# Read-out transpose at step 6 in place of step 3, and a batch's two fp32 subtractions on VectorE in place of GpSimd

## The chip, the core and the metric

One core of one Trainium2 chip. The metric is device time in microseconds of one execution; a version's time is the median of several. The engines are named as in the profile: PE is TensorE (PEld its weight loads), DVE is VectorE, ACT is ScalarE, POOL is GpSimd, SP the engine whose queue issues most of the output transfers and all transposing ones.

## What is computed

Eight batches of cross attention between 512 rows `x` and 32 rows `state` (8 heads of 64), both ways, and a two-layer network with an exact GELU on all 544 rows of each batch:

```python
def _attn_ref(x, state):                       # x [8,8,512,64], state [8,8,32,64]
    a  = softmax(scale * x @ state.T)          # per batch and head
    xread = a @ state                          # 512 rows
    a2 = softmax(scale * state @ x.T)
    sread = a2 @ x                             # 32 rows
    return concat([xread, sread], axis=2)

def _moe_ref(x, w_in, w_out):                  # x [4352,512], w_in [512,2048], w_out [2048,512]
    h = x @ w_in
    g = 0.5 * h * (1.0 + erf(h / sqrt(2)))
    return g @ w_out
```

(The softmax divides by the sum plus 1e-9 after the maximum is subtracted.) Inputs and output are fp32.

## The kernel before

**The 512 rows.** The read of the state and the first layer are joined: `P = state @ w_in` per batch (`p_mm`, `p_copy`), then `hp = A.T @ P` (`mm1`), with A.T made by a transposing DMA (`atr_dma`, tile AT). ScalarE applies the GELU and writes `g`.

**The second layer** of batches 2 to 7 uses seven products of half-size blocks for the eight of a plain one. The blocks' sums are made by VectorE (`g_sum` for the inputs, `w_sums` for the weights); the seven products are `X(b, name)`, in the order 3, 6, 4, 5, 1, 2, 7, each sixteen matmuls at line 586, and their results are combined with fp32 additions and subtractions: `s3` and `s34` (from 3 and 4), `q` (from 1), `u = s34 - [5]` at line 634, `v = q - [2]` at line 605 (inside `c22`), then `[6] + v` at line 608 and `[7] + u` at line 642 give half of the output columns each. ScalarE copies the results of 5 and 2 out of PSUM (lines 632, 636) straight into the output tile `oh`, from which `u` and `v` read them. `x_out(b, 1)` and `x_out(b, 0)`, 512 KB each, leave through SP's queue. The four PSUM banks of `ps_o` are shared by these results and by `p_ps` of the next batch: `p_run` of step 5 writes banks 0 and 1 and then 3 and 2, the banks that lines 608 and 642 read last.

**The 32 rows.** `sread` forms them with matmuls from the unnormalized exponentials and the rows in `xo` (which carry a column of ones); `sread_out` divides by the sum and writes `srm`; `srt(b)` transposes `srm` on TensorE (tile srT, line 402) and VectorE copies it into XSR (line 405), strided by batch. `mm1_sr`, in round 7 from step 3 on, needs XSR of all batches; its second layer is done by `R(name)` in the same seven products, with rows of all batches at once, and its own `r_u` and `r_v` at lines 721 and 727.

**The rows' layouts.** GpSimd loads a batch's rows (`load_x`), copies them into `x4` (`rearr`, line 218) for the transposing DMA of `xtr_dma`, and into `xo` (`rearr_ones`, line 228). xo of batch b+2 replaces that of batch b, so it waits for the `sr` matmuls of batch b.

**Order.** It is written out by hand: each engine runs its instructions in the program's order. The last loop runs rounds b = 2 to 7 of eight steps p. In round b, step p: two `mm1` of batch b in each step; the product X of batch b-1 in the order 4, 5, 1, 2, 7 at steps 0 to 4 (rounds 3 to 7); the scores of batch b+1 and `sread(b)` at step 1; the normalization `norm` of batch b+1 (the tile `a`, line 347) at steps 2 and 3; `srt(b)` at step 3, ahead of the `mm1` of that step; `atr_dma(b+1)` at step 5; P of batch b+1 at steps 5 and 7; X 3 and 6 of batch b at steps 6 and 7. On GpSimd, in a round: `load_x(b+3)` and the `x4` copies of batch b+2 at step 0, `u` at step 1, the `xo` copies of batch b+2 at step 2, `v` at step 3. `load_x` stops after batch 7, so in round 5 the `x4` copies are not held back by a load ahead of them. On SP, in a round: xT of batch b+2, the two x_out of batch b-1, AT of batch b+1.

After the loop come X 4, 5, 1, 2 of batch 7 interleaved with the seven R products, and last `X7_split`, which does product 7 in two halves and sends each half out as soon as line 662 has added `u`.

The pools that matter: `ps_f` has four PSUM slots (tag f) for hp, scores, sr, srT and some p_ps; `cpool` has one buffer for each of s3, s34, q, u, v; `hpool` one for each half of the output.

Of the kernel before, what the change touches and what calls it, by code (L numbers as in the profile page):

```python
# [12 lines left out]
ALU = mybir.AluOpType  # L13
# [4 lines left out]
def kernel(  # L18
# [8 lines left out]
    nc = tc.nc  # L27

    B, H, S, D = x.shape
# [25 lines left out]
    def otile(shape, name, at=None):  # L55
        if at is None:
            at = turn[0] % 4
            turn[0] += 1
        return ps_o.tile(shape, FP32, name=name, tag=f"o{at}")

    def ftile(shape, name):
        return ps_f.tile(shape, FP32, name=name, tag="f")
# [479 lines left out]
    NH = d_model // 2  # L542
# [22 lines left out]
    xs = {}  # L565
# [8 lines left out]
    def g_q(b, h, k):  # L574
        return gs[b][:, MH * k:MH * k + MH, 256 * h:256 * h + 256]
# [19 lines left out]
    def c_tile(name):  # L595
        return cpool.tile([128, 2, NH], FP32, name=name, tag=name)

    def x_out(b, h):
        rows = out[b * SB:b * SB + S, :].rearrange("(p j) n -> p j n", j=SJ)
        nc.sync.dma_start(out=rows[:, 2 * h:2 * h + 2, :], in_=xs[b, "o", h])  # L600

    def c22(b):
        xs[b, "v"] = c_tile("v")
        o = xs[b, "o", 1]
        nc.gpsimd.tensor_tensor(  # L605
            out=xs[b, "v"], in0=xs[b, "q"], in1=o[:, :, :NH], op=ALU.subtract
        )
        nc.vector.tensor_tensor(out=o[:, :, NH:], in0=xs[b, 3], in1=xs[b, "v"], op=ALU.add)
        x_out(b, 1)

    def X(b, name):
        bank = {"3": 0, "4": 1, "5": 0, "2": 1, "1": 2, "6": 3, "7": 2}[name]
        first = name in "3416"
        if first:
            xs[b, bank] = otile([128, 2, NH], "xp", bank)
        ps = xs[b, bank]
        lhs = {"3": (0, 0), "4": (1, 1)}.get(name)
        lhs = xs[b, "g" + name] if lhs is None else g_q(b, *lhs)
        rhs = {"5": w_q[1][1], "2": w_q[0][0]}.get(name)
        rhs = w_sum[name] if rhs is None else rhs  # L620
        x_mm(ps, lhs, rhs, first)
        if name == "3":
            xs[b, "s3"] = c_tile("s3")
            nc.scalar.copy(out=xs[b, "s3"], in_=ps)
            for h in range(2):
                xs[b, "o", h] = hpool.tile([128, 2, d_model], FP32, name="oh", tag=f"oh{h}")
        elif name == "4":
            xs[b, "s34"] = c_tile("s34")
            nc.vector.tensor_tensor(out=xs[b, "s34"], in0=ps, in1=xs[b, "s3"], op=ALU.add)  # L629
        elif name == "5":  # L630
            o = xs[b, "o", 0][:, :, NH:]
            nc.scalar.copy(out=o, in_=ps)  # L632
            xs[b, "u"] = c_tile("u")
            nc.gpsimd.tensor_tensor(out=xs[b, "u"], in0=xs[b, "s34"], in1=o, op=ALU.subtract)  # L634
        elif name == "2":
            nc.scalar.copy(out=xs[b, "o", 1][:, :, :NH], in_=ps)  # L636
            c22(b)
        elif name == "1":
            xs[b, "q"] = c_tile("q")
            nc.vector.tensor_tensor(out=xs[b, "q"], in0=ps, in1=xs[b, "s34"], op=ALU.add)  # L640
        elif name == "7":
            nc.vector.tensor_tensor(
                out=xs[b, "o", 0][:, :, :NH], in0=ps, in1=xs[b, "u"], op=ALU.add
            )
            x_out(b, 0)
# [10 lines left out]
    def X7_split(b):  # L656
        rows = out[b * SB:b * SB + S, :].rearrange("(p j) n -> p j n", j=SJ)
        o = xs[b, "o", 0]
        for j in range(2):
            ps = xs[b, "x", j]  # L660
            x_mm(ps, xs[b, "g7"], w_sum["7"], False, (j,))
            nc.vector.tensor_tensor(
                out=o[:, j, :NH], in0=ps[:, 0, :], in1=xs[b, "u"][:, j, :], op=ALU.add
            )
            eng = nc.scalar if j else nc.sync
            eng.dma_start(out=rows[:, j, :NH], in_=o[:, j, :NH])

    rs = {}

    def r_q(h, k):  # L670
        return g_sr[:, MH * k:MH * k + MH, 128 * h:128 * h + 128]
# [16 lines left out]
    def R(name):  # L688
        def c_new(n):
            rs[n] = cpool.tile([128, NH], FP32, name="r_" + n, tag="r_" + n)  # L690
            return rs[n]

        bank = {"3": 0, "4": 1, "5": 0, "2": 1, "1": 2, "6": 3, "7": 2}[name]
        first = name in "3416"
        if first:
            rs[bank] = ftile([128, NH], "rp")
        ps = rs[bank]
        lhs = {"3": (0, 0), "4": (1, 1)}.get(name)
        lhs = rs["g" + name] if lhs is None else r_q(*lhs)
        rhs = {"5": w_q[1][1], "2": w_q[0][0]}.get(name)  # L700
        rhs = w_sum[name] if rhs is None else rhs
        for m in range(MH):
            nc.tensor.matmul(  # L703
                ps,
                lhsT=lhs[:, m, :],
                rhs=rhs[:, m, :],
                start=(first and m == 0),
                stop=(m == MH - 1),
                skip_group_check=True,
            )  # L710
        add, sub = ALU.add, ALU.subtract
        if name == "3":
            nc.scalar.copy(out=c_new("s3"), in_=ps)
            for h in range(2):
                rs["o", h] = opool.tile([128, d_model], FP32, name="osb", tag="osb")
        elif name == "4":
            nc.vector.tensor_tensor(out=c_new("s34"), in0=ps, in1=rs["s3"], op=add)
        elif name == "5":
            o = rs["o", 0][:, NH:]
            nc.scalar.copy(out=o, in_=ps)  # L720
            nc.gpsimd.tensor_tensor(out=c_new("u"), in0=rs["s34"], in1=o, op=sub)
        elif name == "1":
            nc.vector.tensor_tensor(out=c_new("q"), in0=ps, in1=rs["s34"], op=add)
        elif name == "2":
            o = rs["o", 1][:, :NH]
            nc.scalar.copy(out=o, in_=ps)
            nc.gpsimd.tensor_tensor(out=c_new("v"), in0=rs["q"], in1=o, op=sub)
        elif name == "6":
            nc.vector.tensor_tensor(out=rs["o", 1][:, NH:], in0=ps, in1=rs["v"], op=add)
            r_out(1)  # L730
        elif name == "7":
            nc.vector.tensor_tensor(out=rs["o", 0][:, :NH], in0=ps, in1=rs["u"], op=add)
            r_out(0)
# [11 lines left out]
    def M(*ms):  # L745
        for m in ms:
            mm1(m // MC, m % MC)
# [112 lines left out]
    u = 17  # L860
# [24 lines left out]
    for b in range(2, B):  # L885
        nb = b + 1
        for p in range(8):
            k = 16 * b + 2 * p
            if p == 1 and nb < B:
                scores(nb, 0)  # L890
                scores(nb, 1)
            if p in (2, 3) and nb < B:
                norm(nb, p - 2)
            if p == 3 and nb + 1 < B:
                xtr_dma(nb + 1)
            if p == 5 and nb < B:
                atr_dma(nb)
            if p == 3:
                srt(b)
            M(k, k + 1)  # L900
            if b == 2:
                for _ in range(2 if p < 4 else 1):
                    if u < 32:
                        U(u)
                        u += 1
            elif p < 5:
                if p == 0:
                    g_sum(b - 1, "5")
                X(b - 1, "45127"[p])
                if p < 3:  # L910
                    g_sum(b - 1, "127"[p])
            if nb == B and 3 <= p < 7:
                for m in range(4 * p - 12, 4 * p - 8):
                    mm1_sr(m)
            if p == 1:
                sread(b)
                sread_out(b)
            if p == 0 and b + 3 < B:
                nc.gpsimd.tensor_copy(out=hold, in_=gs[b][:, 0, 0:1])  # L919
                load_x(b + 3)  # L920
            if p == 0 and nb + 1 < B:
                begin(nb + 1)
                rearr(nb + 1)
            if p == 2 and nb + 1 < B:
                rearr_ones(nb + 1)
            if p == 5:
                g_sum(b, "6")
                if nb < B:
                    p_run(nb, (0, 1), ((0, 1), (3, 2)))
            if p == 6:  # L930
                X(b, "3")
            if p == 7:
                if nb < B:
                    p_run(nb, (2, 3), ((1, 2), None))
                X(b, "6")
    b = B - 1
# [9 lines left out]
        out=out[b * SB:b * SB + S, :].rearrange("(p j) n -> p j n", j=SJ)[:, 0:2, NH:],  # L946
# [8 lines left out]
    R("6")  # L955
    R("7")
    X7_split(b)


# [28 lines left out]
```

The softmax here doesn't subtract the row's maximum and nothing guards it: scores larger than these inputs give would overflow.

## Time and profile before

| What | us |
|---|---|
| median of 5 runs | 212.67 (211.88 to 213.21) |
| the profiled execution, its time | 211.88 |
| its span | 210.1 |
| time around the span | 1.8 |
| PE busy | 200.0 |
| DVE busy | 136.0 |
| ACT busy | 132.9 |
| POOL busy | 66.4 |
| POOL idle before u (line 634), waiting for ACT | 66.9 in 6 |
| POOL idle before v (line 605), waiting for ACT | 15.1 in 6 |
| DVE idle before line 608, waiting for v | 6.1 in 4 |
| u and v, each | 1.27 |
| the XSR copy, each | 0.72 |

The granted TensorE clock was 0.998 of full speed over the execution. The span is the profile's own stretch, from the first recorded instruction to the last; a run's time is a little longer. A row's length is the time for which the engine held the instruction, waits inside the instruction included, so that one operation can have several lengths. Consecutive instructions of one engine overlap slightly: an fp32 operation of 512 elements a partition is recorded with 0.69 and the next one starts 0.60 after it. Times in the chain and in the views by time count from the span's start.

### The profile page before, as it was taken

What the parts mean: (1) busy time and instruction counts of PE and PEld (TensorE: products, weight loads), DVE (VectorE), ACT (ScalarE), POOL (GpSimd) and SP (SyncE); (2) the same over time, 40 slices, a digit from 0 to 9 for tenths busy, and PEclk for the clock granted to TensorE, in tenths of its full rate; (3) what the DMA queues carried; (4) which work ended last, traced back from release to release, by engine and by line L of the source; (5) the groups of instructions that cost most, each with busy time, mean ns of one, the idle gap of its engine ahead of it and who ended that gap; (6) DMA issues with size and microseconds to landing.
All of it is one profiled execution on the core that took longest, in us unless ns stands there. A gap on an engine that the chain in (4) does not pass through costs nothing.

```text
span 210.1 us, 4666 instructions
## 1 busy us (share of the span) xinstructions
PE 200.0 (95%) x1955; PEld 130.4 (62%) x1963; DVE 136.0 (65%) x213; ACT 132.9 (63%) x240; POOL 66.4 (32%) x73
## 2 busy tenths in 40 slices
PE   8699999998999999999999999999999999999990
PEld 7445444453444577756775577567766777788880
DVE  2955675739838559984899558855885552357530
ACT  3854865679794878567956496678758455860110
POOL 8964402482270035600576007300220022000330
PEclk9999999999999999999999999999999999999999
DMA  6999999789285809355883910250016001300115
GB/s 193 198 179 204 206 193 187 171 171 180 36 100 132 221 0 131 74 206 46 110 93 142 185 25 3 89 165 0 2 61 192 3 0 61 142 0 0 53 63 188
DMA packets 37861, 23.14 MB, mean 110 GB/s; under 512 B 21712, under 2 KB 35280, under 8 KB 37840
## 3 DMA queue, kind: packets, MB, share of 16 engines
q0 software_dynamic: 13936, 8.10, 28.2%
q1 hardware_dynamic: 23216, 14.29, 27.5%
q10 hardware_dynamic: 688, 0.46, 0.7%
q8 instruction: 15, 0.25, 0.5%
q14 instruction: 6, 0.05, 0.1%
HBM read 17.30 MB, written 8.91 MB: 125 GB/s over the span
## 4 chain that ended last, share of the span: by engine, by line
PE 77%; DVE 12%; ACT 3%; DMA 3%; issue 1%; POOL 1%; DVEq 0%; ACTq 0%
PE xp L586 27%; PE hp L478 21%; PE op L504 9%; DVE gsum L580 5%; PE p_ps L415 4%; PE hps L519 3%; PE op L532 3%; DMA AT<-a 3%; PE rp L703 3%; DVE a L347 2%; PE warm_ps L146 2%; DVE cs L344 1%; PE sr L378 1%; PE pt L324 1%; ACT g L485 1%
## 5 line engine op out<-in xcount | busy, mean ns | idle before, releaser
L485 ACT ACTIVATE g<-hp 128x512 bf16<-128x512 f32 x124 | 67.6, 603 | 31.4 <-PE hp L478 27.3
L478 PE MATMUL hp<-AT,P 128*128 128x512 bf16 x248 | 64.2, 380 | 0.8 <-DVE XSR L405 0.4
L586 PEld LDWEIGHTS <-gsum 128*128 128x128 bf16 x480 | 46.5, 98 | 11.9 <-issue 2.1
L580 DVE TENSOR_TENSOR gsum<-g 128x2048 bf16<-128x2048 bf16 x30 | 39.4, 1326 | 0.0
L478 PEld LDWEIGHTS <-P 128*128 128x128 bf16 x248 | 22.1, 98 | 21.8 <-issue 4.0
L586 PE MATMUL xp<-ws,gsum 128*128 128x256 bf16 x288 | 34.4, 273 | 0.0
L427 DVE CAST P<-p_ps 128x512 bf16<-128x512 f32 x31 | 20.0, 683 | 16.9 <-PE p_ps L415 16.9
L634 POOL TENSOR_TENSOR u<-s,oh 128x512 f32<-128x512 f32 x6 | 7.6, 1266 | 66.9 <-ACT oh L632 66.9
L504 PE MATMUL op<-w_out_bf,g 128*128 128x512 bf16 x90 | 23.0, 379 | 0.3
L586 PE MATMUL xp<-w_out_bf,gsum 128*128 128x256 bf16 x192 | 22.9, 273 | 0.0
L586 PE MATMUL xp<-ws,g 128*128 128x256 bf16 x192 | 22.9, 273 | 0.0
L586 PEld LDWEIGHTS <-g 128*128 128x128 bf16 x192 | 18.8, 98 | 4.3
L426 ACT CAST P<-p_ps 128x512 bf16<-128x512 f32 x31 | 17.0, 604 | 6.5 <-PE p_ps L415 6.5
L504 PEld LDWEIGHTS <-g 128*128 128x128 bf16 x96 | 9.1, 98 | 11.5 <-issue 1.1
L218 POOL COPY x<-xb 128x1024 bf16<-128x1024 bf16 x12 | 12.6, 1081 | 10.6 <-DMA xb<-in_x_dram 10.6
L228 POOL COPY xo<-xb 128x1024 bf16<-128x1024 bf16 x12 | 14.5, 1242 | 1.3 <-PE sr L378 1.3
L347 DVE TENSOR_TENSOR a<-e,ics 128x512 bf16<-128x512 bf16 x14 | 13.9, 995 | 0.5
L629 DVE TENSOR_TENSOR s<-xp,s 128x512 f32<-128x512 f32 x6 | 4.1, 691 | 12.9 <-PE xp L586 12.9
L605 POOL TENSOR_TENSOR v<-q,oh 128x512 f32<-128x512 f32 x6 | 7.7, 1275 | 15.1 <-ACT oh L636 15.1
L344 DVE TENSOR_REDUCE cs<-e 128x16 f32<-128x512 bf16 x14 | 9.5, 676 | 3.8 <-ACT e L331 3.8
L415 PE MATMUL p_ps<-w_in_bf,sbd 64*32 64x512 bf16 x248 | 11.1, 382 | 0.8 <-ACT g L485 0.7
L919 POOL COPY hold<-g 128x1 bf16<-128x1 bf16 x3 | 1.0, 329 | 31.6 <-ACT g L485 31.6
(103 smaller groups left out, 215.7 us busy)
## 6 DMA issues: line engine op xcount, KB each, us to landing
out_dram<-oh SPq DMA_DIRECT2D x11, 512.0 KB, 2.7
xb<-in_x_dram POOLq DMA_DIRECT2D x7, 512.0 KB, 6.8
out_dram<-osb SPq DMA_DIRECT2D x9, 256.0 KB, 3.3
w_out_bf<-in_moe_w_out_dram POOLq DMA_DIRECT2D x4, 512.0 KB, 12.5
w_in_bf<-in_moe_w_in_dram POOLq DMA_DIRECT2D x6, 256.0 KB, 11.3
x0f<-in_x_dram SPq DMA_DIRECT2D x3, 256.0 KB, 3.8
w_in_bf<-in_moe_w_in_dram POOLq DMA_DIRECT2D x4, 128.0 KB, 3.7
x0f<-in_x_dram ACTq DMA_DIRECT2D x1, 256.0 KB, 4.2
```

What stands on the lines that cost most here:

```text
L218: nc.gpsimd.tensor_copy(out=A.x4[:, :, :, 64 * t:64 * t + 64].rearrange("p j c d -> p c j d"), in_=src[:, t],)
L228: eng.tensor_copy(out=A.xo[:, :, :, 2 + 64 * t:66 + 64 * t].rearrange("p j c d -> p c j d"), in_=src[:, t],)
L344: nc.vector.reduce_sum(out=cs, in_=e4, axis=AX.X)
L347: nc.vector.tensor_tensor(out=A.a[:, :, hs].rearrange("p g (c n) -> p g c n", n=NS), in0=e4, in1=ics[:, :, :].to_broadcast((128, G, 2, NS) ...
L415: nc.tensor.matmul(ps[t][32 * c:32 * c + 32, :], lhsT=sbd[64 * t:64 * t + 64, b, c, 32 * t:32 * t + 32], rhs=w_in_bf[64 * t:64 * t + 64, c ...
L426: nc.scalar.copy(out=dst[:, 0, :], in_=ps[0])
L427: nc.vector.tensor_copy(out=dst[:, 1, :], in_=ps[1])
L478: nc.tensor.matmul(hp, lhsT=Ps[b][:, t, m * 128:(m + 1) * 128], rhs=atts[b].AT[:, :, t, :], start=(t == 0), stop=(t == 1),)
L485: nc.scalar.activation(out=gs[b][:, m, :], in_=hp, func=AF.Gelu)
L504: nc.tensor.matmul(ps, lhsT=gs[b][:, m, j * 128:(j + 1) * 128], rhs=w_out_bf[:, m, :], start=(m == 0), stop=(m == MC - 1),)
L580: nc.vector.tensor_tensor(out=t, in0=g_q(b, h0, k0), in1=g_q(b, h1, k1), op=op)
L586: nc.tensor.matmul(ps[:, j - js[0], :], lhsT=lhs[:, m, 128 * j:128 * j + 128], rhs=rhs[:, m, :], start=(first and j == js[0] and m == 0), ...
```

## The change

`srt(b)` of the last loop moves from step 3 to step 6, except in round 7. In both steps it stands ahead of the `mm1` of the step. `u` and `v` of a batch are formed on VectorE, not GpSimd, and both stand in `c22`, which also has line 608's addition and x_out(b, 1); `c22` is no longer called behind product 2 but ahead of the matmuls of product 7 (in `X` and, for the last batch, in `X7_split`). `r_u` and `r_v` are formed on VectorE at their old places. GpSimd is left with the loads and the copies of the rows.

```diff
     def c22(b):
+        xs[b, "u"] = c_tile("u")
+        nc.vector.tensor_tensor(
+            out=xs[b, "u"], in0=xs[b, "s34"], in1=xs[b, "o", 0][:, :, NH:], op=ALU.subtract
+        )
         xs[b, "v"] = c_tile("v")
         o = xs[b, "o", 1]
-        nc.gpsimd.tensor_tensor(
+        nc.vector.tensor_tensor(
             out=xs[b, "v"], in0=xs[b, "q"], in1=o[:, :, :NH], op=ALU.subtract
         )
         nc.vector.tensor_tensor(out=o[:, :, NH:], in0=xs[b, 3], in1=xs[b, "v"], op=ALU.add)
...
         ps = xs[b, bank]
+        if name == "7":
+            c22(b)
         lhs = {"3": (0, 0), "4": (1, 1)}.get(name)
...
         elif name == "5":
             o = xs[b, "o", 0][:, :, NH:]
             nc.scalar.copy(out=o, in_=ps)
-            xs[b, "u"] = c_tile("u")
-            nc.gpsimd.tensor_tensor(out=xs[b, "u"], in0=xs[b, "s34"], in1=o, op=ALU.subtract)
         elif name == "2":
             nc.scalar.copy(out=xs[b, "o", 1][:, :, :NH], in_=ps)
-            c22(b)
...
     def X7_split(b):
         rows = out[b * SB:b * SB + S, :].rearrange("(p j) n -> p j n", j=SJ)
         o = xs[b, "o", 0]
+        c22(b)
         for j in range(2):
...
         elif name == "5":
             o = rs["o", 0][:, NH:]
             nc.scalar.copy(out=o, in_=ps)
-            nc.gpsimd.tensor_tensor(out=c_new("u"), in0=rs["s34"], in1=o, op=sub)
+            nc.vector.tensor_tensor(out=c_new("u"), in0=rs["s34"], in1=o, op=sub)
...
             nc.scalar.copy(out=o, in_=ps)
-            nc.gpsimd.tensor_tensor(out=c_new("v"), in0=rs["q"], in1=o, op=sub)
+            nc.vector.tensor_tensor(out=c_new("v"), in0=rs["q"], in1=o, op=sub)
...
                 atr_dma(nb)
-            if p == 3:
+            if p == (3 if nb == B else 6):
                 srt(b)
```

## The prediction

> Times below are those of the profiled execution (211.88 us, of which the span is 210.1); a "round" is one pass of the last loop, round b working at steps p = 0 to 7 on the scores of batch b and the outputs of batch b-1.
>
> **What bounds the kernel now.** I read the shares first, then the chain of waits, then VectorE and GpSimd in order of time, then the end.
>
> ```profile
> PE 200.0 (95%) x1955; PEld 130.4 (62%) x1963; DVE 136.0 (65%) x213; ACT 132.9 (63%) x240; POOL 66.4 (32%) x73
> PE 77%; DVE 12%; ACT 3%; DMA 3%; issue 1%; POOL 1%; DVEq 0%; ACTq 0%
> ```
>
> TensorE is the bound on the whole, but a chain that is 12% VectorE says that somewhere it is not. The chain shows where: in rounds 3 and 4.
>
> ```profile
> 88.29 1.26 DVE a L347
> 89.55 0.65 DVE XSR L405
> 90.24 0.59 PE hp L478 x2
> 90.83 0.92 PE p_ps L415 x16
> ...
> 111.68 0.73 DVE XSR L405
> 112.45 0.59 PE hp L478 x2
> 113.04 0.92 PE p_ps L415 x14
> 113.96 6.19 DMA AT<-a
> 120.20 1.04 PE hp L478 x4
> ...
> 135.27 0.56 PE p_ps L415 x16
> ```
>
> Columns are start, length, what. In rounds 3 and 4 the second hp of step 5 waits for the XSR copy, and the sixteen p_ps matmuls take 0.92 where those of round 5 take 0.56: their second half needs the two banks that L608 and L642 read last. Round 4 then waits for the AT transfer. The first product of a round (X "4") starts at 76.46, 98.63, 121.24, 142.68 and 164.12, so rounds 3 to 6 last 22.17, 22.61, 21.44 and 21.44. Rounds 5 and 6 are full TensorE work; what is lost is 0.73 in round 3 and 1.17 in round 4, 1.90 in all. Nothing else in the loop can be gained.
>
> VectorE and GpSimd in round 3 (start, length, line):
>
> ```profile
> 78.86 2.52 DVE L580 TENSOR_TENSOR gsum<-g 128x2048 bf16<-128x2048 bf16 x1
> 81.29 1.21 DVE L580 TENSOR_TENSOR gsum<-g 128x2048 bf16<-128x2048 bf16 x1
> 83.82 1.57 DVE L347 TENSOR_TENSOR a<-e,ics 128x512 bf16<-128x512 bf16 x1
> 88.29 1.26 DVE L347 TENSOR_TENSOR a<-e,ics 128x512 bf16<-128x512 bf16 x1
> 89.81 0.89 DVE L608 TENSOR_TENSOR oh<-xp,v 128x512 f32<-128x512 f32 x1
> 90.62 0.67 DVE L642 TENSOR_TENSOR oh<-xp,u 128x512 f32<-128x512 f32 x1
> ...
> 83.81 2.48 POOL L228 COPY xo<-xb 128x1024 bf16<-128x1024 bf16 x2
> 87.73 1.27 POOL L605 TENSOR_TENSOR v<-q,oh 128x512 f32<-128x512 f32 x1 [1.43 <-ACT oh L636]
> ```
>
> The same operation has two lengths: gsum 2.52 or 1.21, a 1.57, 1.26 or 0.69 (its least). The long ones begin while GpSimd is at work; a VectorE operation with both inputs in SBUF stands still until GpSimd's instruction ends (a at 88.29 waits for v, which ends at 89.0). Those that read PSUM (L629, L640) keep their 0.69 beside the same copies.
>
> **The change part by part.**
>
> *XSR to step 6.* The copy leaves the queue between a and L608, where it costs about 0.55 (a ends 89.55, L642 starts 90.62, L608 alone would take 0.60 from start to next start). It lands behind the two P copies of step 5, where VectorE now idles 2.15, 2.08, 2.34 and 2.38 in rounds 3 to 6; that idle time hides its 0.72. Without it the second P pair would be 0.72 late, against about 1.4 of slack left. The slot of srT is next taken by a p_ps of step 7, at 95.33 against an XSR ending near 94: no wait. SP issues nothing for this step. In round 7 it stays at step 3.
>
> *The subtractions.* Per batch, u and v leave GpSimd (1.27 each) and join VectorE in front of L608. The trace has no fp32 subtraction from SBUF on VectorE. Nearest above is GpSimd's 1.27, nearest below half of VectorE's bf16 copy of 1024 (0.71), 0.35; I take 0.69, the row of L608 and L629 with equal shape and type, 0.60 from start to start. Behind the second a, the queue is u 0.60, v 0.69 (L608 must wait for its end), a gap of 0.03, L608 0.60, L642 0.67, less 0.08 overlap: L642 ends 2.51 after a. Now it is 1.74 (89.55 to 91.29), so 0.77 is added. Queued behind are gsum and the P copies; those who wait are p_ps and, through SP's order, x_out, AT and the next xT.
>
> *GpSimd emptied.* u stood in front of the xo copies, which now start when the sr matmuls end.
>
> Round 3: sr ends 81.65, gsum holds until 82.45, xo runs 82.45 to 84.4. The first a, ready at 83.82, ends 85.05 (was 85.39); gsum at 85.57 meets no copy and takes 1.21 (was 1.46); the second a runs 87.69 to 88.38 with no v beside it, 1.17 earlier. L642 ends 88.38 + 2.51 = 90.89, 0.40 earlier. TensorE is at p_ps's second half at 90.61, so still waits; it follows L642 as now: gain 0.40.
>
> Round 4: the same first part, but GpSimd goes on. Before, the copies x of batch 7 (L218) came behind v at 111.15, beside operations that read PSUM. Now they follow xo at once, as their input has landed (issued 99.62, landing after 6.1). The first a ends near 107.30 (was 107.60); if it goes ahead of the copy, that runs to 108.25, gsum (ready 107.82) ends 109.35, the second copy runs to 110.33, the second a (ready 110.26) ends 110.95, 0.80 earlier. L642 ends 2.51 on, at 113.46 against 113.51: 0.05. With round 3 the next round starts 0.45 earlier. The wait for AT moves along, since SP issues AT behind L642's output: L642's end to the first hp of round 5 stays 6.7 (113.51 to 120.20).
>
> Who goes first is the one thing that decides here. At 78.86 gsum waited for both x copies, though the second was issued only at 79.24; at 83.82, 127.93, 129.78 and 110.50 VectorE went in between. I take the four. The Trainium skill (SBUF — State Buffer, "Who interferes with whom") says that whoever issues first holds the shared ports for the whole instruction and the other fully blocks; by it gsum at 78.86 should have gone before the second copy and been near 1.6, where the row has 2.52. By the page the round is the 0.05 gain; by that row it loses one copy, 1.03.
>
> Rounds 5 and 6: L642 at 135.13 and 156.45 against 135.18 and 156.58: the wait for v (0.52, 0.60) pays for most of u and v. TensorE has slack: nothing. Round 7: v now waits 4.47 on GpSimd for ACT; L642 waits for X "7" anyway: nothing.
>
> *The end.*
>
> ```profile
> 203.18 0.42 DVE L729 TENSOR_TENSOR osb<-rp,r_v 128x256 f32<-128x256 f32 x1
> 203.25 0.33 SPq L600 DMA_DIRECT2D out_dram<-oh  x1
> 203.68 1.31 SPq L683 DMA_DIRECT2D out_dram<-osb  x2
> 204.85 0.42 DVE L662 TENSOR_TENSOR oh<-xp,u 128x256 f32<-128x256 f32 x1 [0.45 <-PE xp L586]
> 205.31 0.36 ACTq L666 DMA_DIRECT2D out_dram<-oh  x1
> ```
>
> u, v and L608 of the last batch now stand behind the last row sum, which needs the R products' end (202.9): 202.95 + 0.34 (L732), u to 203.89, v ending 204.58, L608 204.61 to 205.30, L662 at 205.21 and 205.55, ending 205.97 against 205.27: 0.70 later. The 512 KB x_out goes out at 205.35, not 203.25, behind the 2x256 KB of rows instead of ahead. Now the transfers of the end run without a pause from 204.0 to 207.8 at about 380 GB/s, so the last piece waits in line. After: 768 KB from 206.05 (issue + 0.7, as now) take 2.0, to 208.05, 0.2 later than now; if nothing of the line is saved, 0.70 later. The 256 KB transfer of L945, alone, landed in 2.1, so the last issue at 206.03 can't land before 208.1 (now 208.3). I take 0.3, bounds 0 to 0.7. R's two subtractions (0.42 each) lie in idle time (1.87 and 2.73).
>
> *Sum.* -0.40 - 0.05 + 0.30 = -0.15: 211.73 for that execution. It was the fastest of the five; on the median, 212.67 - 0.15 = 212.5. If u and v took 0.35 each, L642 would be 0.6 to 0.7 earlier in both rounds (about -1.2 and a shorter end, near 211.1); at 1.27, 1.2 later in each, +2.4, which I hold unlikely, as L629, L640 and L642 all read 0.67 to 0.69.
>
> **The rivals.**
>
> *Slower: the x copies of batch 7 go ahead of VectorE in round 4.* Place: a or gsum after the first sr of round 4; price 1.03 for one copy; it decides as soon as one copy passes a waiting operation, since L642 has no slack in that round. 212.5 + 1.03 = 213.5. For it speaks gsum at 78.86 and its twin at 101.02 (2.60); against it the four others. The end at its full 0.7 adds 0.4 (213.9).
>
> *Faster: L642 stops being the bound.* If xo and x pass in VectorE's times on PSUM and the pair costs less than 0.77, rounds 3 and 4 come down to 21.44: -1.90 + 0.30, 211.1. For it: the chain runs through XSR and a by name, both of which get shorter. Against: 2.51 behind a is longer than 1.74.
>
> *Nothing in the loop, only the end* (XSR's wait is replaced exactly by u and v): 212.67 + 0.3 = 213.0, inside the forecast's range.
>
> **How the numbers follow.** About 0.3% (0.64) is what this kernel's times can tell from no change. The forecast, with the third rival, has 0.40 (its own range 212.0 to 213.2), the slower rival 0.33, the faster 0.27. Faster by over 0.3%: 0.25 of the faster rival and 0.03 of the forecast, 0.28; slower: 0.29 and 0.04, 0.33; the rest, 0.39, is within. The range reaches to 211.1 (stalls gone) and 213.9 (one copy ahead and the full end).
>
> **What would show it.** Right: rounds 3 and 4 last about 21.8 and 22.5; no wait for XSR; L642 ends 2.5 behind the second a; the first xo starts as gsum ends; x_out of the last batch issued two us later and the last L662 0.7 behind where it stood from TensorE's end. Wrong: a gsum or a of 2.2 or more in round 4 with two copies in a row beside it (slower rival); p_ps of 0.56 in rounds 3 and 4 (faster); u or v far from 0.69; a P copy of step 7 that waits for XSR.

## The result, and the profile after

| | before | changed |
|---|---|---|
| median, us | 212.29 (211.65 to 213.58, 50 runs) | 213.39 (212.75 to 214.80, 29 runs) |
| ratio, 95% interval | | 1.0053 [1.0041, 1.0065] |
| profiled execution: time, span | 211.88, 210.1 | 213.95, 212.2 |
| first scores matmul of round 3 | 78.05 | 78.91 |
| round 3, scores to scores | 22.16 | 21.70 |
| round 4 | 22.61 | 23.61 |
| round 5 | 21.44 | 21.44 |
| round 6 on, to the last matmul's end | 60.56 | 60.56 |
| last matmul's end to the span's end | 5.28 | 5.98 |

The changed kernel is slower by 0.5%, 1.1 us; the forecast was 0.15 less. The rows of the table split the span's 2.1: 0.86 lies before round 3, -0.46 is round 3, +1.00 round 4, +0.70 the end. The 0.86 is not the change's: at the first scores matmuls, far ahead of the last loop, 0.60 of it is there (21.21 against 20.61), and 0.87 at the second ones (46.07 against 45.20). Up to there TensorE of the changed kernel waited 0.7 for the weights `w_out`, which both kernels load alike. Over the kernels profiled below round 3's scores start anywhere from 77.79 to 79.23, and at 80.50 in one execution whose granted clock was 0.83 in the first 20 us. Without the 0.86, 1.24 is left, against 1.10 between the medians. A round is counted here from its first scores matmul (line 324). The span is given to 0.1, so the last row, and what is worked out from it, holds to about 0.05.

Below are the shares and parts of the chain, as the prediction shows them of the kernel before. The columns of the chain are start, length and what ran; line 645 of the changed kernel is 642 of the one before, and 612 is 608.

```profile
PE 201.0 (95%) x1955; PEld 131.1 (62%) x1963; DVE 141.7 (67%) x227; ACT 132.9 (63%) x240; POOL 48.8 (23%) x59
PE 74%; DMA 9%; DVE 7%; POOL 4%; ACT 2%; issue 1%; DVEq 0%; POOLq 0%; ACTq 0%
```

```profile
88.70 1.75 PE xp L586 x16
90.44 0.86 PE hp L478 x4
91.31 0.81 PE p_ps L415 x16
...
101.50 4.80 DVE gsum L580 x2
...
112.23 0.68 DVE u L604
112.92 0.61 DVE v L609
113.59 0.57 issue
114.16 0.69 DVE oh L645
114.90 0.40 PE p_ps L415 x5
115.30 6.25 DMA AT<-a
121.60 1.04 PE hp L478 x4
```

XSR is gone from the chain, the four hp of step 5 run without a gap (0.86), and round 3's p_ps takes 0.81, not 0.92. Round 3's chain now stays on TensorE; before, it ran through VectorE from the first gsum on. In round 4 it still runs through VectorE from there on: the pair of gsum takes 4.80 of it, and u and v follow behind the second a, until it reaches AT as before. GpSimd lost 17.6 of its busy time and VectorE took only 5.7 on: a smaller sum of both, and a slower kernel.

VectorE and GpSimd of the changed kernel in round 4, in order of time (start, length, engine, line):

```profile
101.42 2.91 DVE L580 TENSOR_TENSOR gsum<-g 128x2048 bf16<-128x2048 bf16 x1
104.25 2.06 DVE L580 TENSOR_TENSOR gsum<-g 128x2048 bf16<-128x2048 bf16 x1
107.62 1.11 DVE L347 TENSOR_TENSOR a<-e,ics 128x512 bf16<-128x512 bf16 x1
109.26 1.45 DVE L580 TENSOR_TENSOR gsum<-g 128x2048 bf16<-128x2048 bf16 x1
111.62 0.69 DVE L347 TENSOR_TENSOR a<-e,ics 128x512 bf16<-128x512 bf16 x1
112.23 0.68 DVE L604 TENSOR_TENSOR u<-s,oh 128x512 f32<-128x512 f32 x1
112.84 0.69 DVE L609 TENSOR_TENSOR v<-q,oh 128x512 f32<-128x512 f32 x1
...
100.35 0.87 POOL L117 DMA_DIRECT2D xb<-in_x_dram  x1 [0.67 <-POOL hold L923]
101.22 2.02 POOL L218 COPY x<-xb 128x1024 bf16<-128x1024 bf16 x2
104.17 1.06 POOL L228 COPY xo<-xb 128x1024 bf16<-128x1024 bf16 x1 [0.93 <-PE sr L378]
105.17 2.04 POOL L228 COPY xo<-xb 128x1024 bf16<-128x1024 bf16 x1
107.15 2.48 POOL L218 COPY x<-xb 128x1024 bf16<-128x1024 bf16 x2
```

The same place in the kernel before, where u keeps the xo copies back and v the x copies of batch 7:

```profile
101.02 2.60 DVE L580 TENSOR_TENSOR gsum<-g 128x2048 bf16<-128x2048 bf16 x1
104.81 1.26 POOL L634 TENSOR_TENSOR u<-s,oh 128x512 f32<-128x512 f32 x1 [2.27 <-ACT oh L632]
106.03 2.48 POOL L228 COPY xo<-xb 128x1024 bf16<-128x1024 bf16 x2
111.15 2.48 POOL L218 COPY x<-xb 128x1024 bf16<-128x1024 bf16 x2
```

In the changed kernel the second gsum (of product 2) begins at 104.25, the first xo copy at 104.17. The copy is 0.08 ahead, and the sum takes 2.06 instead of 1.21: it stands until the copy ends near 105.2. Then the second copy stands until the sum has ended, and the x copies of batch 7 follow at once and lengthen the first a (1.11) and the next gsum (1.45). In round 3 of the same execution the sum was first:

```profile
82.15 1.21 DVE L580 TENSOR_TENSOR gsum<-g 128x2048 bf16<-128x2048 bf16 x1
82.47 1.80 POOL L228 COPY xo<-xb 128x1024 bf16<-128x1024 bf16 x1 [1.33 <-PE sr L378]
```

There the copy is the one that stands (1.80 for 1.04), and VectorE loses nothing.

The end of the changed kernel (VectorE, SP and ScalarE's queue):

```profile
204.51 0.42 DVE L736 TENSOR_TENSOR osb<-rp,r_u 128x256 f32<-128x256 f32 x1 [0.39 <-PE rp L707]
204.85 0.68 DVE L604 TENSOR_TENSOR u<-s,oh 128x512 f32<-128x512 f32 x1
205.45 0.69 DVE L609 TENSOR_TENSOR v<-q,oh 128x512 f32<-128x512 f32 x1
206.17 0.69 DVE L612 TENSOR_TENSOR oh<-xp,v 128x512 f32<-128x512 f32 x1
206.78 0.74 DVE L666 TENSOR_TENSOR oh<-xp,u 128x256 f32<-128x256 f32 x2
...
204.18 1.33 SPq L687 DMA_DIRECT2D out_dram<-osb  x2
206.88 0.34 SPq L600 DMA_DIRECT2D out_dram<-oh  x1
207.55 0.36 ACTq L670 DMA_DIRECT2D out_dram<-oh  x1
```

The last matmul ends at 206.22. The three operations stand between the last row sum and the last two additions, which end at 207.52, 1.30 behind the matmul; before it was 0.45.

### The profile page after: what moved, and what is told of

Its sections match the earlier page's. It is cut to its first block, busy times and chain, and to the rows that moved or that the text cites. A ratio compares the mean times of both kernels' runs of the same rounds, so it can differ in the third digit from the quotient of the medians.

```text
span 212.2 us, 4653 instructions
## 1 busy us (share of the span) xinstructions
PE 201.0 (95%) x1955; PEld 131.1 (62%) x1963; DVE 141.7 (67%) x227; ACT 132.9 (63%) x240; POOL 48.8 (23%) x59
## 4 chain that ended last, share of the span: by engine, by line
PE 74%; DMA 9%; DVE 7%; POOL 4%; ACT 2%; issue 1%; DVEq 0%; POOLq 0%; ACTq 0%
PE xp L586 29%; PE hp L478 21%; PE op L504 9%; DMA w_out_bf<-in_moe_w_out_dram 6%; PE p_ps L415 4%; PE hps L519 3%; DMA AT<-a 3%; DVE gsum L580 3%; PE rp L707 3%; POOL w_in_bf L105 2%; PE op L532 2%; PE sr L378 1%; PE pt L324 1%; POOL sbd L95 1%; ACT g L485 1%
## 5 line engine op out<-in xcount | busy, mean ns | idle before, releaser
L580 DVE TENSOR_TENSOR gsum<-g 128x2048 bf16<-128x2048 bf16 x30 | 40.1, 1350 | 0.0
L478 PEld LDWEIGHTS <-P 128*128 128x128 bf16 x248 | 22.5, 98 | 19.6 <-issue 1.3
L228 POOL COPY xo<-xb 128x1024 bf16<-128x1024 bf16 x12 | 13.9, 1192 | 21.7 <-PE sr L378 21.7
L347 DVE TENSOR_TENSOR a<-e,ics 128x512 bf16<-128x512 bf16 x14 | 11.2, 799 | 0.5
L640 ACT COPY oh<-xp 128x512 f32<-128x512 f32 x6 | 3.5, 585 | 9.7 <-PE xp L586 5.1
```

The lines of the kernel that those rows point to most:

```text
L228: eng.tensor_copy(out=A.xo[:, :, :, 2 + 64 * t:66 + 64 * t].rearrange("p j c d -> p c j d"), in_=src[:, t],)
L347: nc.vector.tensor_tensor(out=A.a[:, :, hs].rearrange("p g (c n) -> p g c n", n=NS), in0=e4, in1=ics[:, :, :].to_broadcast((128, G, 2, NS) ...
L478: nc.tensor.matmul(hp, lhsT=Ps[b][:, t, m * 128:(m + 1) * 128], rhs=atts[b].AT[:, :, t, :], start=(t == 0), stop=(t == 1),)
L580: nc.vector.tensor_tensor(out=t, in0=g_q(b, h0, k0), in1=g_q(b, h1, k1), op=op)
```

## The experiments

Each kernel was timed in five turns against the kernel before (the fifth experiment in three), which was timed anew each time (212.32 to 212.67). Rounds 3 and 4 and the end are those of one profiled execution, counted as in the table above; the times and ratios are those of all runs.

**1. The end as before.** The loop is the changed one; in the last batch u and v go back to their old places and to GpSimd, and the rows' two subtractions back to GpSimd (parts of the edit, against the changed kernel).

```diff
         elif name == "5":
             nc.scalar.copy(out=o, in_=ps)
+            if b == B - 1:
+                sub_u(b, nc.gpsimd)
         elif name == "2":
             nc.scalar.copy(out=xs[b, "o", 1][:, :, :NH], in_=ps)
+            if b == B - 1:
+                c22(b)          # v on GpSimd
...
     def X7_split(b):
-        c22(b)
```

> The changed kernel, but the last batch's u and v and the rows' r_u and r_v are formed where they were before and on GpSimd; the loop is as changed. Theory (the end costs 0.87: span less the last matmul's end is 6.14 against 5.27): 0.9 us less than the changed kernel, ratio to before near 1.001, last matmul to span's end near 5.3. Rival (the end costs the 0.3 that was forecast, the rest of the loss is in round 4): 0.3 less, ratio 1.004.

Measured: 212.90 against 212.32, ratio 1.0022 [1.0002, 1.0043]; rounds 3 and 4 21.71 and 23.68, end 5.28. The end's 0.70 is gone and no more: 0.5 us of the change's 1.1 by the medians, 0.6 by the profiled executions, lie in the end, and the rest stays. (The 6.14 and 5.27 of the expectation are 5.98 and 5.28 as counted in the table, so the gain to be had was 0.70, not 0.87.)

**2. No xo copy ahead of the sum of product 2.** On the changed kernel, GpSimd first reads one column of that sum.

```diff
             if p == 2 and nb + 1 < B:
+                if b > 2:
+                    nc.gpsimd.tensor_copy(out=hold, in_=xs[b - 1, "g2"][:, 0, 0:1])
                 rearr_ones(nb + 1)
```

> The changed kernel, with one tiny GpSimd copy ahead of the xo copies of rounds 3 to 5 that reads the block sum of product 2, so that no xo copy can start before that sum is made. Theory (in round 4 an xo copy that started 0.08 ahead of this sum held it up by 0.9, and that is the loss of the round): round 4 falls from 23.6 to about 22.5, the sums take 1.21 each behind the x copies, ratio about 1.0005. Rival (the loss of round 4 is u and v themselves, in front of the two last additions): round 4 stays above 23, ratio 1.005. Third: the profiled execution was a rare one; then the median moves by less than half of the 1.0.

Measured: 213.55 against 212.32, ratio 1.0059 [1.0033, 1.0084]; rounds 22.09 and 23.23. The theory was too simple. VectorE and GpSimd of this kernel in round 4:

```profile
100.69 4.06 DVE L580 TENSOR_TENSOR gsum<-g 128x2048 bf16<-128x2048 bf16 x2
106.07 1.50 DVE L347 TENSOR_TENSOR a<-e,ics 128x512 bf16<-128x512 bf16 x1
...
104.87 0.19 POOL L930 COPY hold<-gsum 128x1 bf16<-128x1 bf16 x1 [2.35 <-DVE inv L391]
105.00 2.03 POOL L228 COPY xo<-xb 128x1024 bf16<-128x1024 bf16 x2
106.96 3.48 POOL L218 COPY x<-xb 128x1024 bf16<-128x1024 bf16 x2
```

The pair of sums falls from 4.89 to 4.06, so the order at 104 did cost 0.83. But the copies held back run 105.0 to 107.0, and the first a takes 1.50 where it took 1.11. Round 4 gains 0.38, round 3, which had no such loss, gives back 0.39 in the same way. The copies are only moved along VectorE's queue.

**3. The read-out transpose alone.** The kernel before with one condition:

```diff
-            if p == 3:
+            if p == (3 if nb == B else 6):
                 srt(b)
```

> The kernel before, with the read-out transpose alone at step 6. Theory (the XSR copy costs about 0.55 of VectorE's queue ahead of the last additions in rounds 3 and 4, and hides at step 6): rounds 3 and 4 near 21.65 and 22.0, 1.0 us less than before, ratio 0.995. Rival (the gain is only the wait that names XSR, 0.17 and 0.21): 0.4 less, ratio 0.998.

Measured: 211.07 against 212.32, ratio 0.9944 [0.9924, 0.9963]; rounds 21.59 and 22.02. VectorE's queue, round 3, behind the second a and around XSR:

```profile
88.05 1.20 DVE L347 TENSOR_TENSOR a<-e,ics 128x512 bf16<-128x512 bf16 x1
89.17 0.68 DVE L608 TENSOR_TENSOR oh<-xp,v 128x512 f32<-128x512 f32 x1
89.77 0.68 DVE L642 TENSOR_TENSOR oh<-xp,u 128x512 f32<-128x512 f32 x1
...
92.70 0.72 DVE L405 COPY XSR<-srT 128x128 bf16<-128x128 bf16 x1
94.98 1.29 DVE L427 CAST P<-p_ps 128x512 bf16<-128x512 f32 x2 [1.56 <-PE p_ps L415]
```

The additions follow a directly, and XSR stands where VectorE still idles 1.56 behind it. This half of the change is a gain of 1.2 us.

**4. The subtractions alone.** The changed kernel with `if p == 3: srt(b)` back.

> The changed kernel with the read-out transpose back at step 3: the subtractions' move alone. Theory (u and v add 0.77 behind the second a, gain 1.17 ahead of it in round 3, and the end costs 0.87): round 3 near 22.3, round 4 near 24, 2.2 us more than before, ratio 1.010. Rival (the read-out's place does nothing when u and v are there): ratio 1.005, as the changed kernel.

Measured: 215.41 against 212.32, ratio 1.0135 [1.0104, 1.0166]; rounds 22.21 and 24.09, round 5 21.77, end 5.97. That is 3.1 us, where 2.2 were expected. With experiment 3 all four combinations of the two parts are there. The table gives the end of the last addition (line 642 or 645), counted from the round's first scores matmul, and the rounds:

| | last addition, round 3 | round 4 | round 3 lasts | round 4 |
|---|---|---|---|---|
| before | 13.24 | 13.30 | 22.16 | 22.61 |
| transpose at 6 | 12.64 | 12.68 | 21.59 | 22.02 |
| subtractions on VectorE | 13.31 | 14.79 | 22.21 | 24.09 |
| both | 12.75 | 14.23 | 21.70 | 23.61 |

With either engine the transpose brings the last addition 0.56 to 0.62 forward and shortens each of the two rounds by 0.48 to 0.59; the subtractions cost about 0.1 in round 3 and 1.5 in round 4. In these two rounds the parts add up. On the whole kernel they do not: -1.25 and +3.09 would make 1.84 of the medians, and both together cost 1.10. The difference lies behind round 4. With XSR, u and v all ahead of the last additions, these come late in rounds 5 and 6 too, and p_ps waits for them there:

```profile
139.19 0.94 PE L415 MATMUL p_ps<-w_in_bf,sbd 64*32 64x512 bf16 x16
```

In the kernel before these sixteen take 0.63 (at 135.20). Round 5 and the stretch from round 6 on are 0.33 and 0.31 longer in experiment 4, and not at all in experiment 3 or in the changed kernel.

**5. GpSimd's copies taken away.** This version of the changed kernel leaves out the xo copies of batches 4 to 7, so the 32 rows of these batches are summed from older rows; the x copies of batch 7 wait for the second a of round 4.

```diff
             if p == 0 and nb + 1 < B:
                 begin(nb + 1)
+                if b + 3 == B:
+                    nc.gpsimd.tensor_copy(out=hold, in_=atts[b].a[:, 0, 64:65])
                 rearr(nb + 1)
-            if p == 2 and nb + 1 < B:
-                rearr_ones(nb + 1)
```

> The changed kernel without the xo copies of batches 4 to 7, so that the 32 rows of these are summed from older rows; the x4 copies of batch 7 are held behind the second a of round 4. This leaves out GpSimd's copies beside the two block sums and the two a. Theory (GpSimd's copies are what round 4 loses, u and v are not): all of these VectorE operations but the first sum are at 1.21 and 0.69, round 4 at most 22.0, below both kernels. Rival (u and v in VectorE's queue are the loss): round 4 stays at 23 or more.

Measured: 211.50, ratio 0.9953 [0.9928, 0.9978], the changed end included; rounds 21.45 and 21.63. With the same u and v in VectorE's queue, round 4 is 1.98 shorter than the changed kernel's: 0.66 for the x copies of batch 7 (experiment 6) and 1.32 for the xo copies. What round 4 lost to is GpSimd's copies; u and v alone would be affordable.

**6. Only the x copies of batch 7 held back.** The `hold` line of experiment 5 on the changed kernel, xo copies kept.

> The changed kernel, with a tiny GpSimd copy ahead of the x4 copies of batch 7 that reads the second a of round 4, so that these copies cannot stand beside the first a and the block sum behind it. Theory (round 4 pays for four GpSimd copies in a row): first a 0.69 in place of 1.11, block sum 1.21 in place of 1.45, round 4 from 23.6 to about 22.9, ratio near 1.002. Rival (only the copy that passes the sum of product 2 counts): round 4 unchanged, ratio 1.005.

Measured: 212.93 against 212.67, ratio 1.0025 [1.0002, 1.0047]; round 4 22.95, the first a 0.69, the gsum behind it 1.21. So of the changed kernel's round 4, 0.66 was these two copies, which v had held back until 111.15 in the kernel before. (The medians tell less of it: 0.26 above the kernel before, where the profiled execution shows 0.58.)

**7. The end: place or engine.** Experiment 1 with the three operations and the rows' subtractions on VectorE, at the old places.

> The changed kernel, but in the last batch u stands behind product 5 and v and the addition behind product 2, on VectorE; only the place in the queue differs from the changed kernel there. Theory (the end's 0.70 is the place: the three stand between the last row sum and the last two additions): last matmul's end to span's end back to 5.28 from 5.98, 0.65 us less than the changed kernel, ratio near 1.002. Rival (it is the engine): 5.98 stays, ratio 1.005.

Measured: 212.63 against 212.67, ratio 1.0006 [0.9979, 1.0034]; rounds 21.71 and 23.68; the last matmul ends at 205.97, the span at 210.8: 4.83. That is below the 5.28 of the kernel before. The place was the loss of the end. The engine there is a gain in the profiled execution: v takes 0.69, not 1.27, and x_out is issued 2.19 ahead of the last matmul's end, not 1.57.

**8. AT ahead of the output transfers.** On experiment 3:

```diff
-            if p == 5 and nb < B:
+            if p == 3 and nb < B:
                 atr_dma(nb)
```

> The kernel before with the read-out transpose at step 6, and the AT transfer issued at step 3, ahead of the two output transfers on SP. Theory (AT is late in round 4 because it stands behind x_out, which waits for the last addition): the wait of 0.2 to 0.4 at the start of round 5 goes, round 4 near 21.65, 0.4 us less than with the transpose alone, ratio 0.9925. Rival (AT then meets xT or the loads and is as late): ratio 0.994 to 0.996.

Measured: 210.91 against 212.67, ratio 0.9930 [0.9906, 0.9954]; rounds 21.59 and 21.64. AT lands 3.1 after its issue, not 6.2, and the wait at the start of round 5 is gone. In this kernel SP takes AT at 110.95, as soon as the second a is written (110.89), and not behind line 642.

**9. The best parts together.** Experiment 8, with only the last batch's u and v and the rows' two subtractions on VectorE at their old places.

```diff
     def c22(b):
-        nc.gpsimd.tensor_tensor(
+        eng = nc.vector if b == B - 1 else nc.gpsimd
+        eng.tensor_tensor(
...
         elif name == "5":
-            nc.gpsimd.tensor_tensor(out=xs[b, "u"], ...
+            eng = nc.vector if b == B - 1 else nc.gpsimd
+            eng.tensor_tensor(out=xs[b, "u"], ...
```

> The kernel before with the read-out transpose at step 6, AT issued at step 3, and only the last batch's u, v and the rows' two subtractions on VectorE, at their old places. Theory (the end gains where VectorE idles: with these places last matmul to span's end was 4.83, against 5.28 on GpSimd): rounds 3 and 4 at 21.6, end 4.8, 0.45 less than with the first two edits alone, ratio near 0.991. Rival (the end's 4.83 was one execution's): 0.993.

Measured: 210.57 against 212.61, ratio 0.9888 [0.9855, 0.9922]; rounds 21.59 and 21.63, end 4.82. It beats both kernels.

**10. The change mended.** The changed kernel with the old places at the end (on VectorE), the x copies of batch 7 held back and AT at step 3.

> The changed kernel with what the runs found wrong around it mended: the last batch's three operations at their old places (on VectorE), the x4 copies of batch 7 held behind the second a of round 4, AT issued at step 3. u and v of the loop stay on VectorE. Theory (u and v on VectorE still cost round 4 what the xo copies cost that u no longer holds back, and 0.77 behind the second a): round 4 near 22.5, about 0.9 above the 21.64 of the version with GpSimd's u and v, ratio near 0.9955. Rival (once mended, the move to VectorE is as good): round 4 near 21.7, ratio 0.991.

Measured: 211.68 against 212.61, ratio 0.9946 [0.9921, 0.9971]; rounds 21.71 and 22.55, end 4.92. Round 4 stays 0.92 above experiment 9's. It has the same sum of 2.06 again (4.91 for the pair of gsum): the xo copies still start when the sr matmuls end. Experiment 5, which has u and v at the same places and no xo copies, has 3.71 for the pair and a round 4 of 21.63.

Whether rounds and end account for the times: what the profiled executions show against the kernel before (rounds 3 to the last matmul, and the end, summed) beside the difference of the medians, both in us.

| kernel | rounds and end | medians |
|---|---|---|
| the changed kernel | +1.24 | +1.10 |
| 1, end as before | +0.61 | +0.58 |
| 2, xo behind the sum | +1.27 | +1.23 |
| 3, transpose alone | -1.16 | -1.25 |
| 4, subtractions alone | +2.85 | +3.09 |
| 5, no xo copies | -1.05 | -1.17 |
| 6, x of batch 7 held | +0.58 | +0.26 |
| 7, end on VectorE, old places | +0.17 | -0.04 |
| 8, AT first | -1.54 | -1.76 |
| 9, best parts | -2.00 | -2.04 |
| 10, mended | -0.87 | -0.93 |

All agree within 0.35, so nothing large lies ahead of round 3. From round 3 on the differences are in rounds 3 and 4 and the end, but for the 0.64 of experiment 4 in rounds 5 and 6.

## Why the prediction was wrong

*What failed first: "Round 4: the same first part".* The step took over from round 3 that the gsum of product 2 runs when the sr matmuls end, so that the xo copies must wait for it. In the changed kernel's round 4 the gsum before it ended only near 104.3, the sr matmuls near 104.2 (ends of matmuls are modelled), so GpSimd was ready first: its copy began 0.08 before the sum. The margin was small already: in the kernel before, that gsum ended at 103.62 and sr at 103.81, 0.19 apart, and u stood ahead of xo so that it didn't matter. What used it up is 0.33 by which GpSimd issued the load of the round later (0.67 behind the hold copy instead of 0.33); the x copies behind the load, and with them the end of the first gsum, came 0.31 later in the round. The second a was forecast to end 0.80 earlier in the round; counted from the scores it ended at 11.70 against 11.54, 0.16 later. That 0.96, less the 0.05 of gain forecast for the last addition, makes 0.91 of the 0.93 that it came later (14.23 against 13.30), and the round lasted 1.00 longer. Of the 0.96, 0.31 is the later load and 0.85 the stand of the sum (2.06 for 1.21); the first a and the gsum behind it took 0.19 less than forecast (1.11 and 1.45 for 1.22 and 1.53). The order alone would not have saved the forecast: with the sum first (experiment 2) the copies stand beside the first a, and round 4 still lasts 23.23, where about 22.5 was forecast.

*The rival.* The slower rival had the mechanism (a GpSimd copy goes ahead of a VectorE operation in round 4, at about one copy's length) and nearly the time (213.5; 213.39 was measured), but another place, and in part by luck: its one copy was priced at 1.03, and the 0.96 above is the stand of a sum and a later load together, while the end lost 0.70, not the 0.30 in its sum. It looked at the x copies of batch 7, against the first a and the gsum behind it. There VectorE did go in between: the a of 1.11 waited for the rest of one copy, not for both. The copy that went ahead was xo. The Trainium skill (SBUF — State Buffer, "Who interferes with whom") says that the order of issue decides who blocks; that would have named the place, had the prediction asked which of the two is ready first there, and not only who wins once both wait. The trace agrees with it at 104.17 (copy first, sum 2.06) and at 82.15 (sum first, copy 1.80); it does not at the first gsum of rounds 3 and 4: that of round 4 began at 101.42, ahead of the second x copy, and took 2.91, so it stood until both had ended at 103.24.

*The end: mis-sized.* The additions' delay was worked out as 0.70 (it was 0.85), and the span's end moved by 0.70, the upper bound given; 0.30 was taken, as the transfers were thought to run on without a pause, so that the last piece would wait in line either way. They did not. (Their rate before was also read too high, as about 380 GB/s: the 1.31 MB of 204.0 to 207.8 make 345.) In steps of half a microsecond (the fields: stretch, length, busy of PE, PEld, DVE, ACT, POOL, granted clock, DMA share, GB/s):

```profile
206.50:207.00 0.50, 0.00 (x0) 0.00 (x0) 0.50 (x2) 0.00 (x0) 0.00 (x0) 1.00 1.04 373
207.00:207.50 0.50, 0.00 (x0) 0.00 (x0) 0.50 (x2) 0.00 (x0) 0.00 (x0) 1.00 0.42 156
207.50:208.00 0.50, 0.00 (x0) 0.00 (x0) 0.02 (x1) 0.00 (x0) 0.00 (x0) 1.00 0.59 246
208.00:208.50 0.50, 0.00 (x0) 0.00 (x0) 0.00 (x0) 0.00 (x0) 0.00 (x0) 1.00 1.01 401
```

The rows' two transfers were through before x_out began, at half share between 207.0 and 208.0, and the last piece landed 2.8 after its issue where it took 3.0 before: 0.2 was saved of a delay of 0.85. Experiments 1 and 7 show that it is the place of the three operations.

*What held.* u and v took 0.68 and 0.69, and from the second a's end to the last addition's 2.53 (2.51 forecast; 112.31 to 114.84). Round 3: the last addition 0.49 earlier (0.40 forecast), the round 0.46 shorter. L645's end to round 5's first hp: 6.76 (6.7). XSR at step 6 delays nothing; rounds 5 and 6 lose nothing. The transpose itself was priced at about 0.55 in each round; the last addition came 0.56 to 0.62 sooner by it.

Why GpSimd's load came 0.33 later in round 4 of the kernels that keep the xo copies and have no v behind them (experiments 1, 4, 6, 7 and 10; in 2 the hold copy itself came 0.35 later; not 3, 5, 8 and 9) is open; no run here shows the cause.

## What to carry to other kernels

An operation on a side engine can be worth more by what it holds back than it costs: u and v, 1.27 each and off the chain, held four copies back where VectorE set the pace: two until the sum of product 2 was made, two until the second a was at work. Before emptying an engine, ask what moves up, what it will stand beside, and which of the two will be ready first, with the margin in hundredths of a microsecond. A bundle of edits should be timed apart: here one condition was worth -1.25 us alone and the other half +3.09, and together they cost 1.10, not the sum of 1.84.

## What was not expected of the hardware

The first gsum of round 3, which begins 0.6 behind the start of the first of two GpSimd copies, waits for both (2.52 in both kernels, beside x copies that take 2.02). An a that begins with the first of two gets in between (1.57, the second copy then 1.50), and so does the gsum that begins 0.08 behind the first xo copy (2.06, the second copy then 2.04). What decides which of the two goes next is not shown. The transposing transfer AT of round 4 landed 3.1 after its issue when it went ahead of the two 512 KB output transfers (experiment 8), and 6.2 behind them (the kernel before).
